# Linear attention beside a squared-ReLU MLP: the reciprocal denominators reach their features by DMA through DRAM instead of by matmuls, and three S groups run in one burst

## The chip, the cores and the metric

The kernel runs on one core of a Trainium2 chip. The metric is device time in microseconds of one execution. TensorE does the matmuls, VectorE and ScalarE read the results out of PSUM, GpSimd (POOL) does adds in SBUF, and SyncE (SP) issues nearly all DMA transfers. PSUM has eight banks of 128 partitions by 512 f32 values, and SBUF holds everything else.

## The reference

The input x is [2048, 448] in bf16. It is normalised per token, without scale or shift, and the result goes into two branches:

```
xn  = layernorm(x)
q, k, v = xn @ wqkv, 16 heads of 28 features;  phi(t) = where(t > 0, t + 1, exp(t)) + 1e-6
kv  = sum over s of phi(k)[s, d] * v[s, e]      per head
z   = sum over s of phi(k)[s, d]                per head
den = phi(q) . z + 1e-6                         per token and head
s   = ((phi(q) @ kv) / den) @ wo
h   = relu(xn @ w1 + b1) ** 2 ;  g = silu(h @ w2 + b2)      1792 hidden features
out = x + s * g
```

There is one denominator for each token and head, 2048 x 16 numbers. Each divides the 28 features of phi(q) of that head, so before the division a number has to be copied to 28 features. That copying is what the change is about.

## The kernel before, in words

**Tiles.** The 2048 tokens are 16 tiles of 128, in four groups of 512. The 448 features are three chunks of 128 and a rest of 64. phi(q) is kept transposed, features on partitions: chunks 0 to 2 in `pqT` (128 x 3 x 2048), the rest in `pqx`, where partitions 0 to 63 hold the even tiles and 64 to 127 the odd ones. phi(k) is kept with tokens on partitions, in `pk`.

**Stages.** The first half normalises, transposes, and runs three kinds of units with the transposed input `xT`: K units (L624, one token tile of phi(k)), Q units (L650, a chunk of phi(q) for one group) and H units (L716, 128 hidden features for one group; L683 adds the bias and takes the ReLU, L697 or L698 squares, into `r2`). Units are packed by fours (`quads`, `pe_four`), two at a time on 64 rows each of the array. Then the attention is folded:

- `qx` (L664) makes the rest features of phi(q); `token_sum` (L785, L791) multiplies xn and phi(k) over all tokens into `at`; `z_cols` (L838) makes z.
- `den` (L883, L890) multiplies phi(q) by z into one bank: partition 32g + h holds head h of token group g. ScalarE takes the logarithm (L905) and exp of its negative (L909): `rden`, the reciprocal denominators, 512 tokens per row.
- `spread(c)` (L921, L927) copies them to features: for each group a matmul of 32 rows of a 0/1 matrix `ehd` with `rden` gives a bank in which each feature's row is its head's row. VectorE multiplies phi(q) by the four banks, in place (L944).
- `fold_wv` (L813) and `fold_wo` (L861) turn `at` into one 448 x 448 matrix `msb`, so that the attention's output is phi(q)/den times `msb`.

Last comes the output, tile by tile. A **gate tile**, `gg(si)` (L957), is 14 matmuls of 448 columns; VectorE evicts it with the bias into `gbuf` (L966), ScalarE applies silu (L999). An **S group**, `ss4` or `ss4_rests_last` (L1026), makes the attention output of four tiles in four banks with 28 matmuls, two at a time. `gate` multiplies an S bank by `gbuf` into `obuf` (L1009), POOL, or VectorE for the last tiles, adds x (L1015), and SP stores the tile. Tiles 12 to 15 are made by `s_tails` (L1082, the rest features, which opens four banks) and `s_main` (L1099). Tile 15 is made in two halves of 224 columns (`gg_part`, L977, L979).

**What sets the order.** Every operation is recorded by `add` with the names it reads and writes, and `schedule` plans all of them on five queues with assumed durations. TensorE and SP keep the order in which the program lists them; on the other engines the planner picks the order. It also gives each PSUM result a bank. Each operation waits for its inputs by semaphores, and every engine works strictly in its planned order. TensorE's list from `den` on is: four H units of group 3, spread 0, fold_wv, gate tile 4, spread 1, fold_wo, tile 5, spread 2, tiles 6 and 7, spread 3, S groups 0 and 1, tiles 8 to 14, S group 2, tails, mains of tiles 12 to 14, tile 15 in halves.

Of the kernel before, what the change touches and what calls it, by code (L numbers as in the profile page):

```python
# [6 lines left out]
ALU = mybir.AluOpType  # L7
AF = mybir.ActivationFunctionType

P = 128  # L10
S, D, F = 2048, 448, 1792
NT, NG, NF = S // 128, S // 512, F // 128
NH, DH = 16, 28
HC = 4
PD = 112
NGB, NOB = 8, 8

LAT = 0.12
PSUM_BANKS = 8
# [280 lines left out]
def bass_recurrent_scan__linear_attn_block__dense_activation_squared_relu__prompt_kernel(  # L300
    nc, A_x, A_wqkv, A_wo, B_x, B_w1, B_b1, B_w2, B_b2, out
):
    with ExitStack() as es:
# [8 lines left out]
        zmask = sb("zmask", [P, 5, 32], f32)  # L312
        ones = sb("ones", [P, 1], bf)
        wz = sb("wz", [P, P], bf)
        ehd = sb("ehd", [P, D], bf)
        x_tok = sb("x_tok", [P, NT, D], bf)
        wqh = sb("wqh", [P, 64], bf)
        xn = sb("xn", [P, NT, 512], bf)
# [19 lines left out]
        eps5 = sb("eps5", [P, 1], f32)  # L338
        r2 = sb("r2", [P, NF, S], bf)
        kvm = sb("kvm", [P, 4, D], bf)  # L340
        msb = sb("msb", [P, 4, D], bf)
        zsb = sb("zsb", [P, 5, 32], bf)
        lnd = sb("lnd", [P, 512], f32)[:, :]
        rden = sb("rden", [P, 512], bf)
# [9 lines left out]
        def free_ap(ap, dims):  # L354
            return bass.AP(tensor=ap.tensor, offset=ap.offset, ap=[ap.ap[0]] + dims)
# [16 lines left out]
        def vset(ap, val, name, again=False, dur=0.08):  # L372
            add("dve", lambda e, _: e.memset(ap, val), [name] if again else [], [name], dur)
# [2 lines left out]
        pr.ops[-1].prio = -1e6  # L376
        vset(hmask[:, :], 1.0, "hmask", dur=0.15)
        vset(zmask[:, :, :], 1.0, "zmask", dur=0.2)
        vset(ehd[:, :], 0.0, "ehd", dur=0.3)
        vset(kvm[:, :, :], 0.0, "kvm", dur=1.0)  # L380
        pool(lambda e, _: e.memset(ones[:, :], 1.0), ["ones"], dur=0.1)
        pool(lambda e, _: e.memset(eps6[:, :], 1e-6), ["eps6"], dur=0.1)
# [12 lines left out]
        def head_masks(after):  # L395
            hv = hmask[:, :].rearrange("p (b j) -> p b j", b=HC)
            select(hv, "hmask", [[-DH, HC], [0, DH]], 0, 1, 0.0, after=after)
            select(hv, "hmask", [[DH, HC], [0, DH]], DH - 1, -1, 0.0, after=after)
            ev = ehd[:, :].rearrange("p (h j) -> p h j", h=NH)
            for g in range(NG):  # L400
                select(ev, "ehd", [[-1, NH], [0, DH]], -32 * g, 1, 1.0, ALU.not_equal, dur=0.6, after=after)

        tok = lambda t, lo, hi: t[0].rearrange("(p s) d -> p s d", s=NT)[:, lo:hi, :]

        def dma(eng, dst, src, writes, nbytes, reads=(), dur=0.45):
            op = add(eng, lambda e, _: e.dma_start(dst, src), reads, writes, dur, nbytes=nbytes)
            if eng == "act":
                op.prio = -1000.0 + len(pr.ops)
# [442 lines left out]
        def fold_wo(c):  # L851
            b = Buf("M")
            hs = {0: (0, 1), 1: (1, 2), 2: (2, 3), 3: (3,)}[c]

            def f(e, _):
                last = None
                for o in range(1 if c < 3 else 2):
                    dst = ps(b)[:, 0:D] if c < 3 else ps(b)[64 * o : 64 * o + 64, 0:D]
                    wd = P if c < 3 else 64
                    for h in hs:  # L860
                        last = e.matmul(  # L861
                            dst, kvm[0:PD, h, c * P : c * P + wd], w_o[0:PD, h, :], start=(h == hs[0]),
                            stop=(h == hs[-1]),
                        )
                return last

            add("pe", f, ["kvd", "kvm", "wo"], [b], 0.19 * len(hs) * (2 if c == 3 else 1))

            def ev(e, eng):
                if eng == "dve":  # L870
                    return e.tensor_copy(msb[:, c, :], ps(b)[:, 0:D])
                return e.activation(out=msb[:, c, :], in_=ps(b)[:, 0:D], func=AF.Copy)

            add("dve", ev, [b], [("msb", c)], 0.62, alts=[("act", 0.55)])

        denb = Buf("DEN")

        def den():
            def f(e, _):
                last = None  # L880
                for c in range(3):
                    for g in range(NG):
                        last = e.matmul(  # L883
                            ps(denb)[32 * g : 32 * g + 32, 0:512], zsb[:, c, :], pqT[:, c, g * 512 : (g + 1) * 512],
                            start=(c == 0), stop=False, skip_group_check=True,
                        )
                for o in (0, 1):
                    for g in range(NG):
                        d4 = ps(denb)[32 * g : 32 * g + 32, o * P : o * P + P]
                        last = e.matmul(  # L890
                            free_ap(d4, [[2 * P, 2], [1, P]]), zsb[:, 3 + o, :],
                            pqx[:, g // 2, 2 * (g % 2) : 2 * (g % 2) + 2, :], start=False, stop=(o == 1),
                            skip_group_check=True,
                        )
# [13 lines left out]
            add(  # L908
                "act", lambda e, _: e.activation(out=rden[:, :], in_=lnd, func=AF.Exp, scale=-1.0), ["lnd"],  # L909
                ["rden"], 0.65,  # L910
            )

        def spread(c):
            bufs = [Buf("RB") for _ in range(NG)]

            def f(e, _):
                last = None
                for g in range(NG):
                    r = slice(32 * g, 32 * g + 32)
                    if c < 3:  # L920
                        last = e.matmul(  # L921
                            ps(bufs[g])[:, 0:512], ehd[r, c * P : (c + 1) * P], rden[r, :], start=True, stop=True
                        )
                    else:
                        for o in (0, 1):
                            d4 = rden[r, o * P : o * P + P]
                            last = e.matmul(  # L927
                                ps(bufs[g])[64 * o : 64 * o + 64, 0:256], ehd[r, 384:448],
                                free_ap(d4, [[2 * P, 2], [1, P]]), start=True, stop=True,
                            )  # L930
                return last

            add("pe", f, ["rden", "ehd"], bufs, 0.22).mode = "row32"
            for g in range(NG):
                if c < 3:
                    sl, n, nm = pqT[:, c, g * 512 : (g + 1) * 512], 512, ("pq", g, c)
                    rd, wr = [nm], [nm]
                else:
                    sl = pqx[:, g // 2, 2 * (g % 2) : 2 * (g % 2) + 2, :].rearrange("p a b -> p (a b)")
                    n = 256  # L940
                    rd, wr = [("pqx", g // 2)], [("pqy", g)]
                add(
                    "dve",
                    lambda e, _, sl=sl, b=bufs[g], n=n: e.tensor_tensor(  # L944
                        out=sl, in0=sl, in1=ps(b)[:, 0:n], op=ALU.mult
                    ),
                    [bufs[g]] + rd, wr, 0.68 if c < 3 else 0.41,
                )

        def gg(si):  # L950
# [265 lines left out]
        for i in range(12, 16):  # L1216
            zsum(i)
        quads("Q2.0 H3.4 Q2.1 H3.6 Q2.2 H3.5 Q3.0 H3.7 Q3.1 H3.12 Q3.2 H3.13")
        qx(0)
        qx(1)  # L1220
        token_sum(3)
# [2 lines left out]
        z_cols()  # L1224
        token_sum(2)
        den()
        quads("H3.8 H3.9 H3.10 H3.11")
        silu_set()
        for si in range(4):
            silu(si)  # L1230
# [25 lines left out]
        s_main(us[3], 3, True, 0, 224)  # L1256
        gg_part(15, 224, D)
# [31 lines left out]
```

## Time and profile before

The median of three executions is 146.9 us (146.82 to 147.07). One more execution was profiled:

| | |
|---|---|
| time of the profiled execution | 146.83 us |
| its span, first to last instruction | 145.1 us |
| granted TensorE clock | 1.0 |
| busy: TensorE, VectorE, ScalarE, POOL | 140.2, 95.7, 78.2, 36.5 us |
| time by queue, of 16 DMA engines | SP's 26.6%, ACT's 0.2% |

The span leaves out 1.7 us around the instructions. Matmuls are pipelined, so the mean of one in the profile (353 ns for 448 columns) is longer than the distance from one to the next; durations of stages are better taken from the chain of work that ended last, which lists stretches without overlap.

### The profile page before, as it was taken

What the parts mean: (1) busy time and instruction counts of PE and PEld (TensorE: products, weight loads), DVE (VectorE), ACT (ScalarE), POOL (GpSimd) and SP (SyncE); (2) the same over time, 40 slices, a digit from 0 to 9 for tenths busy, and PEclk for the clock granted to TensorE, in tenths of its full rate; (3) what the DMA queues carried; (4) which work ended last, traced back from release to release, by engine and by line L of the source; (5) the groups of instructions that cost most, each with busy time, mean ns of one, the idle gap of its engine ahead of it and who ended that gap; (6) DMA issues with size and microseconds to landing.
All of it is one profiled execution on the core that took longest, in us unless ns stands there. A gap on an engine that the chain in (4) does not pass through costs nothing.

```text
span 145.1 us, 2851 instructions
## 1 busy us (share of the span) xinstructions
PE 140.2 (97%) x1134; PEld 72.5 (50%) x1134; DVE 95.7 (66%) x218; ACT 78.2 (54%) x150; POOL 36.5 (25%) x55
## 2 busy tenths in 40 slices
PE   7999999999999999999999999999999999999990
PEld 7774444444455444444444454464444455554490
DVE  5869989899985177678999500089847913123792
ACT  3618897988884198869879412598411012212010
POOL 2123025470000487003540000000000991000590
PEclk9999999999999999999999999999999999999999
DMA  3977899920744100000000000000000232000034
GB/s 94 315 240 234 209 183 374 340 84 0 52 97 103 41 5 0 0 0 5 2 0 0 5 0 0 0 5 2 0 0 0 65 104 88 0 0 0 5 127 127
DMA packets 16025, 10.53 MB, mean 73 GB/s; under 512 B 7500, under 2 KB 15628, under 8 KB 16012
## 3 DMA queue, kind: packets, MB, share of 16 engines
q1 hardware_dynamic: 15824, 10.28, 26.6%
q8 instruction: 9, 0.15, 0.4%
q10 hardware_dynamic: 188, 0.07, 0.2%
q14 instruction: 4, 0.03, 0.1%
HBM read 6.94 MB, written 1.84 MB: 60 GB/s over the span
## 4 chain that ended last, share of the span: by engine, by line
PE 96%; DVE 1%; ACT 1%; issue 0%
PE pb L957 28%; PE pb L716 26%; PE pb L624 7%; PE pb L785 6%; PE pb L650 6%; PE pb L1026 6%; PE pb L712 3%; PE pb L1114 3%; PE pb L979 2%; PE pb L1099 1%; PE pb L664 1%; PE pb L861 1%; PE pb L791 1%; PE pb L921 1%; PE pb L813 1%; PE pb L883 1%
## 5 line engine op out<-in xcount | busy, mean ns | idle before, releaser
L957 PE MATMUL pb<-w,r 128*128 128x448 bf16 x210 | 40.6, 353 | 0.0
L716 PE MATMUL pb<-xT,w 64*128 64x512 bf16 (+1 forms) x291 | 38.3, 376 | 0.0
L683 ACT ACTIVATE r<-pb,b1f 128x512 bf16<-128x512 f32 x54 | 33.7, 691 | 6.7 <-PE pb L716 6.7
L957 PEld LDWEIGHTS pb<-w,r 128*128 128x128 bf16 x210 | 20.2, 98 | 19.5 <-issue 1.2
L1015 POOL TENSOR_TENSOR obuf<-obuf,x_tok 128x448 bf16<-128x448 bf16 x13 | 13.1, 1043 | 53.9 <-DVE obuf L1009 53.9
L999 ACT ACTIVATE gbuf<-gbuf 128x448 bf16<-128x448 bf16 x15 | 8.3, 579 | 26.2 <-DVE gbuf L966 26.1
L716 PEld LDWEIGHTS pb<-xT,w 64*128 64x128 bf16 (+1 forms) x291 | 14.2, 94 | 16.5 <-ACT r L683 0.4
L966 DVE TENSOR_TENSOR gbuf<-pb,b2b 128x448 bf16<-128x448 f32 x15 | 9.4, 625 | 19.3 <-PE pb L957 19.2
L634 POOL TENSOR_TENSOR zacc<-zacc,pk 128x448 f32<-128x448 f32 x13 | 14.5, 1116 | 18.9 <-DVE pk L614 18.4
L697 DVE TENSOR_TENSOR r<-r 128x512 bf16<-128x512 bf16 x37 | 17.4, 502 | 2.0 <-ACT r L683 1.9
L624 PE MATMUL pb<-w_qkv,xT 64*128 64x448 bf16 x112 | 13.2, 349 | 0.0
L944 DVE TENSOR_TENSOR pqT<-pqT,pb 128x512 bf16<-128x512 bf16 x12 | 7.4, 681 | 7.2 <-PE pb L921 7.2
L602 ACT ACTIVATE pk<-pb 128x448 bf16<-128x448 f32 x16 | 7.8, 541 | 7.7 <-PE pb L624 7.7
L698 ACT ACTIVATE r<-r 128x512 bf16<-128x512 bf16 x19 | 11.2, 633 | 0.0
L650 PE MATMUL pb<-xT,w_qkv 64*128 64x512 bf16 x84 | 11.0, 376 | 0.0
L1009 DVE TENSOR_TENSOR obuf<-pb,gbuf 128x448 bf16<-128x448 f32 (+1 forms) x17 | 9.0, 590 | 2.6 <-PE pb L1026 2.4
L716 PE MATMUL pb<-xT,w_1r 64*128 64x512 bf16 x56 | 10.3, 377 | 0.0
L614 DVE SCALAR_TENSOR_TENSOR pk<-pb,pk 128x448 bf16<-128x448 f32 x16 | 9.9, 624 | 0.5
L466 DVE BATCH_NORM_STATS2 st<-x_tok 128x6 f32<-128x448 bf16 x16 | 9.2, 614 | 1.4 <-DMA x_tok<-in_A_x_dram 1.4
L785 PE MATMUL pb<-pk,xn 128*128 128x448 bf16 x48 | 9.4, 353 | 0.0
L607 DVE TENSOR_SCALAR pk<-pk 128x448 bf16<-128x448 bf16 x16 | 6.0, 377 | 4.3 <-ACT pk L602 4.2
L624 PEld LDWEIGHTS pb<-w_qkv,xT 64*128 64x128 bf16 x112 | 5.4, 94 | 6.1 <-issue 0.4
(92 smaller groups left out, 134.5 us busy)
## 6 DMA issues: line engine op xcount, KB each, us to landing
out_dram<-obuf SPq DMA_DIRECT2D x15, 112.0 KB, 1.7
w<-in_B_w_dram SPq DMA_DIRECT2D x1, 1568.0 KB, 9.5
x_tok<-in_A_x_dram SPq DMA_DIRECT2D x3, 448.0 KB, 4.4
w<-in_B_w_dram SPq DMA_DIRECT2D x3, 384.0 KB, 4.2
w_qkv<-in_A_wqkv_dram SPq DMA_DIRECT2D x3, 336.0 KB, 5.6
w_o<-in_A_wo_dram SPq DMA_DIRECT2D x1, 392.0 KB, 8.9
w_qkv<-in_A_wqkv_dram SPq DMA_DIRECT2D x6, 56.0 KB, 5.1
x_tok<-in_A_x_dram SPq DMA_DIRECT2D x2, 112.0 KB, 2.1
```

The source lines that it names most:

```text
L614: lambda e, _: e.scalar_tensor_tensor(out=slot, in0=ps(buf)[:, 0:n], scalar=1.0 + 1e-6, in1=slot, op0=ALU.add, op1=ALU.max),
L624: return e.matmul(ps(b)[:, 0:D], xT[rw, si, c, :], w_qkv[rw, c, D : 2 * D], start=start, stop=stop)
L634: lambda e, _: e.tensor_tensor(out=o[:, 0:D], in0=pk[:, 0, :] if i == 1 else zacc[:, :], in1=pk[:, i, :], op=ALU.add),
L650: return e.matmul(ps(b)[:, 0:512], w_qkv[rw, c, m * P : (m + 1) * P], xT[rw, 4 * g : 4 * g + 4, c, :], start=start, stop=stop,)
L683: rl = lambda e, _: e.activation(out=slot, in_=ps(b)[:, 0:512], func=AF.Relu, bias=b1f[:, fi : fi + 1])
L697: return e.tensor_tensor(out=slot, in0=slot, in1=slot, op=ALU.mult)
L698: return e.activation(out=slot, in_=slot, func=AF.Square)
L716: return e.matmul(ps(b)[:, 0:512], lhs, xT[rw, 4 * g : 4 * g + 4, c, :], start=start, stop=stop, skip_group_check=not full,)
L785: last = e.matmul(ps(b)[:, 0:D], xn[:, si, c * P : (c + 1) * P], pk[:, si, :], start=(si == 0), stop=(si == NT - 1),)
L957: last = e.matmul(ps(b)[:, 0:D], r2[:, fi, si * P : (si + 1) * P], w_2[:, fi, :], start=(fi == 0), stop=(fi == NF - 1),)
L966: lambda e, _: e.tensor_tensor(out=gbuf[:, si % NGB, :], in0=ps(b)[:, 0:D], in1=b2b[:, :], op=ALU.add),
L1015: lambda e, _: e.tensor_tensor(out=ob, in0=ob, in1=x_tok[:, si, lo:hi], op=ALU.add),
```

## The change

The four spread matmuls and the matrix `ehd` go. `rden` is stored to a DRAM scratch `rden_rows` (16 heads x 2 x 1024: even tiles, then odd ones) by four transfers, one per token group; the Exp that makes `rden` writes the even and odd tiles apart. Twelve transfers then load it back, with each head's row repeated for its 28 features, into the space of `pk`, which nobody needs by then; chunk 0 takes two pieces, chunks 1 and 2 three each, and the rest four, because chunks of 128 cut through heads of 28. VectorE multiplies from there: two operations of 1024 columns for each chunk and two of 512 for the rest, instead of twelve of 512 and four of 256 from PSUM.

TensorE's list changes: the four H units come before `qx` instead of after `den`; after `den` come tile 4, fold_wv, tile 5, fold_wo, tiles 6 to 11; then S groups 0, 1, 2 and the tails in one burst; then tiles 12 to 14 and the mains. `gbuf` gets 12 slots and `obuf` 10; to make room `msb` shares the memory of `at`. All three mains of tiles 12 to 14 now have their add on VectorE. The planner's assumed cost of issuing a DMA goes from 0.45 to 0.6.

```diff
-NGB, NOB = 8, 8
+NGB, NOB = 12, 10
-        ehd = sb("ehd", [P, D], bf)
+        rsp = nc.dram_tensor("rden_rows", [NH, 2, 1024], bf)
-        msb = sb("msb", [P, 4, D], bf)
+        msb = at
-        vset(ehd[:, :], 0.0, "ehd", dur=0.3)
-            ev = ehd[:, :].rearrange("p (h j) -> p h j", h=NH)
-            for g in range(NG):
-                select(ev, "ehd", [[-1, NH], [0, DH]], -32 * g, 1, 1.0, ALU.not_equal, dur=0.6, after=after)
-        def dma(eng, dst, src, writes, nbytes, reads=(), dur=0.45):
+        def dma(eng, dst, src, writes, nbytes, reads=(), dur=0.6):
-            add("dve", ev, [b], [("msb", c)], 0.62, alts=[("act", 0.55)])
+            add("dve", ev, [b], [("msb", c), ("at", c)], 0.62, alts=[("act", 0.55)])
-                "act", lambda e, _: e.activation(out=rden[:, :], in_=lnd, func=AF.Exp, scale=-1.0), ["lnd"],
-                ["rden"], 0.65,
+                "act",
+                lambda e, _: e.activation(
+                    out=rden[:, :].rearrange("p (o j t) -> p j o t", o=2, j=2),
+                    in_=lnd.rearrange("p (j o t) -> p j o t", o=2, j=2), func=AF.Exp, scale=-1.0,
+                ),
+                ["lnd"], ["rden"], 0.65,
-        def spread(c):
...
+        rb = pk[:, :, :].rearrange("p a b -> p (a b)")
+        def store_rden():
+            for g in range(NG):
+                dma(
+                    "sp", rsp.ap()[:, :, g * 256 : (g + 1) * 256],
+                    rden[32 * g : 32 * g + NH, :].rearrange("p (o x) -> p o x", o=2), [("rd", g)], NH * 1024, ["rden"],
+                )
+        def load_rden(c):
+            done = [o for o in pr.ops if o.eng in ("pe", "pool") and any(r in o.reads for r in [("pk", NT - 1)])]
+            def piece(p0, h, n, reps, cols, src0, name):
+                src = bass.AP(tensor=rsp, offset=h * 2048 + src0, ap=[[2048, n], [0, reps], [1, cols]])
+                o = 2048 * c
+                dma("sp", rb[p0 : p0 + n * reps, o : o + cols], src, [name], n * reps * cols * 2, [("rd", g) for g in range(NG)])
...
+            for half in range(1 if c < 3 else 2):
...
+                while f < f1:
+                    h = f // DH
+                    n = (f1 - f) // DH if f % DH == 0 else 0
+                    reps = DH if n else min((h + 1) * DH, f1) - f
...
+                    piece(p0 + f - f0, h, n, reps, cols, src0, ("rb", c, half, k))
...
+        def divide(c):
+            for v in (0, 1):
+                if c < 3:
+                    sl = pqT[:, c, v * 1024 : (v + 1) * 1024].rearrange("p (j o t) -> p j o t", o=2, t=P)
+                    o = 2048 * c + v * 512
+                    r = free_ap(rb[:, o : o + P], [[P, 4], [1024, 2], [1, P]])
...
+                else:
+                    sl = pqx[:, v, :, :].rearrange("p a b -> p (a b)")
+                    r = rb[:, 6144 + 512 * v : 6656 + 512 * v]
...
+                    "dve", lambda e, _, sl=sl, r=r: e.tensor_tensor(out=sl, in0=sl, in1=r, op=ALU.mult), rd + names[c], wr,
...
         quads("Q2.0 H3.4 Q2.1 H3.6 Q2.2 H3.5 Q3.0 H3.7 Q3.1 H3.12 Q3.2 H3.13")
+        quads("H3.8 H3.9 H3.10 H3.11")
         qx(0)
...
         den()
-        quads("H3.8 H3.9 H3.10 H3.11")
+        store_rden()
+        for c in range(4):
+            load_rden(c)
         silu_set()
...
-        spread(0)
+        ggs(4)
         fold_wv()
-        ggs(4)
-        spread(1)
+        ggs(5)
         for c in range(4):
             fold_wo(c)
-        ggs(5)
-        spread(2)
         ggs(6)
-        ggs(7)
-        spread(3)
-        ss4_rests_last(0)
+        for si in range(7, 12):
+            ggs(si)
+        for c in range(4):
+            divide(c)
+        ss4(0)
         ss4(1)
-        for si in range(8, 15):
-            ggs(si)
         ss4(2)
         us = s_tails([(12, 0, D), (13, 0, D), (14, 0, D), (15, 0, D)])
+        for si in range(12, 15):
+            ggs(si)
         for k in range(3):
-            s_main(us[k], k, k > 0)
+            s_main(us[k], k)
```

More of the change, by code (lines that the diff above doesn't have):

```diff
@@ L908, in den @@
             add(
-                "act", lambda e, _: e.activation(out=rden[:, :], in_=lnd, func=AF.Exp, scale=-1.0), ["lnd"],
-                ["rden"], 0.65,
-            )
-        def spread(c):
[L914 to L933, printed above, removed]
-            for g in range(NG):
+                "act",
@@ new lines, in load_rden @@
+        def load_rden(c):
[4 more added lines that the diff above has]
+                dma("sp", rb[p0 : p0 + n * reps, o : o + cols], src, [name], n * reps * cols * 2, [("rd", g) for g in range(NG)])
+                pr.ops[-1].deps.update(done)
+                for d in done:
+                    d.succ.append(pr.ops[-1])
+            for half in range(1 if c < 3 else 2):
+                f0, p0, k = P * c, 64 * half, 0
+                f1 = f0 + (P if c < 3 else 64)
+                cols, src0 = (2048, 0) if c < 3 else (1024, 1024 * half)
+                f = f0
+                while f < f1:
+                    h = f // DH
+                    n = (f1 - f) // DH if f % DH == 0 else 0
+                    reps = DH if n else min((h + 1) * DH, f1) - f
+                    if f % DH == 0 and n == 0:
+                        reps = f1 - f
+                    n = max(n, 1)
+                    piece(p0 + f - f0, h, n, reps, cols, src0, ("rb", c, half, k))
+                    f += n * reps
+                    k += 1
+                names[c] = names.get(c, []) + [("rb", c, half, i) for i in range(k)]
@@ L935, in spread @@
+        names = {}
+        def divide(c):
+            for v in (0, 1):
                 if c < 3:
-                    sl, n, nm = pqT[:, c, g * 512 : (g + 1) * 512], 512, ("pq", g, c)
-                    rd, wr = [nm], [nm]
-                else:
-                    sl = pqx[:, g // 2, 2 * (g % 2) : 2 * (g % 2) + 2, :].rearrange("p a b -> p (a b)")
-                    n = 256
-                    rd, wr = [("pqx", g // 2)], [("pqy", g)]
-                add(
[L943 to L947, printed above, removed]
+                    sl = pqT[:, c, v * 1024 : (v + 1) * 1024].rearrange("p (j o t) -> p j o t", o=2, t=P)
+                    o = 2048 * c + v * 512
+                    r = free_ap(rb[:, o : o + P], [[P, 4], [1024, 2], [1, P]])
+                    rd = wr = [("pq", g, c) for g in (2 * v, 2 * v + 1)]
+                else:
+                    sl = pqx[:, v, :, :].rearrange("p a b -> p (a b)")
+                    r = rb[:, 6144 + 512 * v : 6656 + 512 * v]
+                    rd, wr = [("pqx", v)], [("pqy", 2 * v), ("pqy", 2 * v + 1)]
+                add(
+                    "dve", lambda e, _, sl=sl, r=r: e.tensor_tensor(out=sl, in0=sl, in1=r, op=ALU.mult), rd + names[c], wr,
+                    0.78 if c < 3 else 0.42,
```

## The prediction

> **What bounds the kernel now.** I read the page's totals first, then the chain of work that ended last.
>
> ```profile
> span 145.1 us, 2851 instructions
> PE 140.2 (97%) x1134; PEld 72.5 (50%) x1134; DVE 95.7 (66%) x218; ACT 78.2 (54%) x150; POOL 36.5 (25%) x55
> PE 96%; DVE 1%; ACT 1%; issue 0%
> ```
>
> TensorE carries 96% of the chain (third line), so a matmul removed is time gained, unless TensorE then waits. Next the chain in order of time (start, us, what) around the edit:
>
> ```profile
> 77.64 1.85 PE pb L664 x16
> ...
> 91.07 0.22 PE pb L890 x8
> 91.29 3.13 PE pb L716 x28
> 94.42 0.33 PE pb L921 x4
> 94.74 0.96 PE pb L813 x16
> 95.70 2.65 PE pb L957 x14
> 98.35 0.33 PE pb L921 x4
> 98.68 1.55 PE pb L861 x8
> 100.23 2.75 PE pb L957 x14
> ...
> 108.72 0.25 PE pb L927 x8
> 108.96 5.45 PE pb L1026 x56
> ...
> 135.81 0.38 PE pb L1082 x4
> 136.19 1.81 PE pb L1099 x9
> 138.00 0.10 PE pb L977
> ```
>
> A gate tile (L957) costs 2.65 us alone and 2.75 after another tiling of the array: each switch costs 0.10. The spreads (L921, L927) stand directly on the chain. Then the tail, from the timeline (start, us):
>
> ```profile
> 137.97 3.16 POOL L1015 TENSOR_TENSOR obuf<-obuf,x_tok 128x448 bf16<-128x448 bf16 x3
> 142.02 0.28 DVE L1015 TENSOR_TENSOR obuf<-obuf,x_tok 128x224 bf16<-128x224 bf16 x1
> 142.99 0.45 SPq L406 DMA_DIRECT2D out_dram<-obuf  x1
> ```
>
> The last add ends at 142.30, but its store is issued at 142.99: SP takes stores in order, and those behind POOL's last add (ended 141.13) go out some 0.48 apart. That is 0.67 us of queue at the end. Last, the DMA part:
>
> ```profile
> q10 hardware_dynamic: 188, 0.07, 0.2%
> out_dram<-obuf SPq DMA_DIRECT2D x15, 112.0 KB, 1.7
> ```
>
> A store lands 1.7 us after its issue. Queue 10 (ACT's) had three transfers: b1r with 14 rows and two w_1r pieces of 64: 142 data packets. The other 46 are 14 + 16 + 16[...].
>
> [...] The trace shows slow matmuls only in the warm-up at the start (36 in 4.02 us)[...]. [...] VectorE's 448-column adds beside POOL took 1,070 ns, the 224-column ones 270.
>
> **The change part by part.** TensorE. Up to 77.64 its order is unchanged. The group of four H units (28 matmuls, 3.13 with its switch, 3.02 without) moves ahead of qx, so den ends at 91.29 + 3.02 = 94.31. Its banks are free by then: the Q phi that holds one of them ended at 76.91. From there, by the rows above: gate tile 4, 2.75; fold_wv 0.86 (0.96 less the switch); tile 5, 2.65; fold_wo 1.45; tiles 6 to 11, 2.75 + 5 x 2.65 = 16.00, ending at 118.02. The S burst: a switch and 84 matmuls, 8.05 (28 took 2.65); tails 0.38; tiles 12 to 14, 8.05; s_main 1.71 without its switch. It ends at 136.2, against 138.0: **1.80 us off TensorE**, of which the spreads are 0.33 x 3 + 0.25 = 1.24 and the rest are switches.
>
> Tail. POOL's last add is now that of tile 11 and ends before tile 14; tiles 12 to 14 are added on VectorE. So SP's queue is empty when the last add ends: **0.67 us** (between 0.4 and 0.7; VectorE gets one full add more, but then has no POOL beside it, and has the last tile's other half to make up lateness).
>
> DMA, all on SP's queue. rden was ready at 92.69 and is now at 95.71. Four stores, 0.5 apart, the last issued at 97.2 and landed 1.7 later: 98.9. All twelve loads wait for all four stores. They bring 384 rows of 4,096 B and 128 of 2,048 B, 1.84 MB. Over 16 engines at the 374 GB/s of the page's fullest slice that is 4.9 us. But the source patterns are 4 heads x 28 copies for chunks 0 and 1, 3 x 28 for chunk 2, 2 x 28 twice for chunk 3, against 112, 84 and 56 partitions[...]. Engine 0 then gets 28+1, 1+28+1 and 2+28+2 rows of 4 KB, 91, and 2 x (1+28) = 58 of 2 KB. The packet records of before show 140 ns for 3,584 B and 74 for 1,792 B; the line through both gives 159 for 4,096 and 83 for 2,048. Sum 91 x 0.159 + 58 x 0.083 = 19.3 us. With 0.9 us from issue to first packet and 0.2 to the semaphore, both read from the output stores' packets, chunk 3 lands at **119.3**; chunks 0, 1, 2 at about 104.7, 109.4, 114.5. Bounds: pipelined packets at the line's slope alone (151 ns) give 118.1; the 3,584 B packets under full load came one per 167 ns and engine, 190 for 4 KB, which gives 123.
>
> VectorE. Removed: 12 multiplies of 681 ns and 4 of 414 from PSUM. Added: six of 128x1024 and two of 128x512, all in SBUF. The nearest row is the 128x512 square, 418 ns[...]. VectorE works in order, and its order in the changed kernel is: chunk 0 both halves, tile 7's eviction, chunk 1 first half, chunk 2 first half, tile 8's eviction, chunk 3's first half (the rest features), chunks 1 and 2 second halves, tile 9's eviction, chunk 3's second half, tiles 10 and 11. So while VectorE waits for chunk 3, the evictions of tiles 9 to 11 queue behind; TensorE doesn't notice, since those three tiles have banks of their own. The first S group needs chunk 3's first half: 119.3 + 0.42 + 0.1 = 119.8, where TensorE is ready at 118.1: **a stall of 1.7 us**. After it VectorE owes 1.3 + 0.62 + 0.4 + 1.24 = 3.6 us and reaches S's first gate at 123.3, 1.2 after that was ready. Gates take 0.57 against TensorE's 0.66 a tile, so it catches up; two bank waits of about 0.1 remain (second S1 pair behind tile 11's eviction, tile 12 behind a gate): 0.2.
>
> At nothing: removing the ehd memset and four selects (POOL 25% busy); msb laid over at (fold_wo writes 3 us after fold_wv read it); gbuf 12 and obuf 10 deep (gates 10 and 11 wait for the stores of tiles 0 and 1, landed some 3 us before); the strided Exp. Their cover is idle time on POOL, ACT and VectorE, and without it each costs below 0.3.
>
> Sum: -1.80 - 0.67 + 1.7 + 0.2 = -0.57. The profiled execution took 146.83, the median is 146.9: **146.3**.
>
> **The rivals.** *All engines serve the loads.* If the split follows the destination's partitions, everything lands by about 108, ten us early: 146.9 - 2.47 = 144.4. [...]
> *Slow few engines, ending slower.* The same wait, but each 4 KB packet takes over about 164 ns, or the twelve transfers leave gaps on engine 0. At 164 the stall, 2.5, eats the whole gain; at 190, chunk 3 lands at 123.0, the stall is 5.5, 144.4 + 5.6 = 150.0[...]. For it: the 167 ns under load, and every engine reads the same row 28 times. Against: only four engines draw on the memory here, where 16 did.
> *The burst is bound by gates.* Twelve tiles need 6.8 us of gates and VectorE enters with tile 11's eviction; if gates slow to over 0.66, tile 12 waits: about 1 us on top of 144.4. The gates of before, beside POOL's adds as here, kept 0.57.
>
> **How the numbers follow.** Forecast 0.48 (own range 145.0 to 147.3), all engines 0.20, slow engines 0.27, gates or another small wait 0.05. The smallest change that a measurement here can tell from none is 0.2%, 146.6 to 147.2. Below it: 0.34 of the forecast, 0.19 and 0.02: 0.55. Within: 0.09, 0.02 and 0.01: 0.12. Above: 0.33, mostly the slow engines. The range goes from 144.2, just below the all-engine case, to 149.5, which leaves the worst of the slow engines, about 0.12, outside.
>
> **What would show it.** Right: TensorE idle 1 to 2.5 us before the first S group, released by VectorE, which waited for the last load; the loads at some 100 GB/s from 100 to 119; landings growing to 10 us and more; the last store issued within 0.1 of the last add. Wrong: loads done by 110 and no idle (first rival), packets well over 160 ns (second), idle inside the burst (third), or idle between den and tile 11, which I put at none.

## The result and the profile after

The changed kernel takes 153.74 us in the median of six executions (152.91 to 154.65), against 146.86 us (146.67 to 147.07) for the kernel before: a ratio of 1.0469, with a 95% interval of 1.0422 to 1.0515. It is slower by 6.9 us. The predicted 146.3 us is wrong, and its range, 144.2 to 149.5, does not hold the result either.

The profiled execution of the changed kernel took 154.65 us, the slowest of the six; what follows is read from it. Line numbers are those of the changed kernel: a gate tile is L975, an S group L1044, a division L964, a DMA issue L402. First the page's totals, the two rows of 40 slices that changed most (a slice is 3.8 us), and the shares of the chain:

```profile
span 152.6 us, 2814 instructions
PE 140.8 (92%) x1114; PEld 73.3 (48%) x1114; DVE 91.3 (60%) x212; ACT 77.1 (51%) x148; POOL 32.8 (22%) x50
PEclk9999999999999999999999999999999965999999
GB/s 94 329 201 222 167 262 373 273 50 24 118 16 122 0 4 0 0 0 4 0 0 4 0 0 0 18 17 108 103 101 77 55 25 4 35 86 150 90 71 53
PE 76%; DMA 10%; SPq 8%; ACT 1%; DVE 1%; issue 1%
```

TensorE was 96% of the chain and is now 76%; transfers and their issue have taken 18%. The granted clock, whose mean was 1.0 before, falls to 0.6 and 0.5 in slices 33 and 34, shortly before and in the S burst. And just before that, the transfer rate comes down in steps, 108, 103, 101, 77, 55, 25 GB/s: by the packet records the loads' packets run mostly four at a time from 108.3 to 114.2, then three to 118.9, then two to 123.2. The chain in order of time (start, us, what) has the whole story:

```profile
95.20 0.64 ACT rden L906
...
97.21 0.59 SPq L402
...
97.84 2.75 DMA rden_rows<-rden
...
100.61 0.74 SPq L402
...
107.90 3.88 SPq L402
...
111.82 13.17 DMA pk<-rden_rows
...
125.01 0.44 DVE pqx L964
...
125.50 10.21 PE pb L1044 x63
...
136.08 8.05 PE pb L975 x42
144.14 1.70 PE pb L1117 x9
```

`rden` is ready at 95.84. Its four stores are issued one after another and the last lands at 100.59. Only then do the twelve loads go out, and the last of them lands at 124.99. The eleventh of these issues took 3.88 us, but the packets of the loads ran on beside it, at 100 to 102 GB/s from 108 to 112. VectorE divides (0.44), and TensorE starts the S burst at 125.50. Tile 11 had ended at 118.10. The waits of TensorE and of VectorE in this stretch (us in total, times, longest) say the same:

```profile
PE pb L1044 <- DVE pqx L964: 7.4, 1, 7.4
DVE pqT L964 <- DMA pk<-rden_rows: 12.2, 3, 4.7
DVE pqx L964 <- DMA pk<-rden_rows: 3.6, 1, 3.6
```

The burst itself, 84 matmuls of which the chain lists 63, then takes 10.21 us; at full clock the same 84 take 8.05, as in the runs below. These stretches (bounds; us; busy time of TensorE, its weight loads, VectorE, ScalarE, POOL; granted clock; DMA share; GB/s) show why:

```profile
121.00:123.00 2.00, 0.00 (x0) 0.00 (x0) 0.43 (x1) 0.58 (x1) 0.00 (x0) 0.99 0.13 49
123.00:125.00 2.00, 0.00 (x0) 0.00 (x0) 0.00 (x0) 0.00 (x0) 0.00 (x0) 0.50 0.07 25
...
127.00:129.00 2.00, 2.00 (x14) 0.86 (x12) 1.57 (x4) 1.50 (x3) 0.00 (x0) 0.50 0.04 8
129.00:131.00 2.00, 2.00 (x20) 0.86 (x16) 1.17 (x3) 0.18 (x1) 0.47 (x1) 0.81 0.00 0
131.00:133.00 2.00, 2.00 (x24) 1.03 (x22) 1.51 (x3) 0.00 (x0) 2.00 (x3) 1.00 0.18 57
```

The last matmul of tile 11 ends at 118.10; by the clock records the granted clock falls to 0.5 at 122.95, after 4.85 idle microseconds, and stays there until 129.78, the first 4.3 us of the burst: 14 matmuls in 2 us where 24 fit at full clock. Last the tail, from the timeline:

```profile
149.85 0.27 DVE L1033 TENSOR_TENSOR obuf<-obuf,x_tok 128x224 bf16<-128x224 bf16 x1
150.16 0.33 SPq L402 DMA_DIRECT2D out_dram<-obuf  x1
```

The last store is issued as soon as the last add has ended.

The two profiled executions differ by 154.65 - 146.83 = 7.82 us. The last S matmul of tiles 12 to 14 ends at 145.84 instead of 138.00, which is +7.84: 7.40 of idle time, 2.16 of half clock (10.21 - 8.05), and -1.72 of TensorE work that is gone. From there to the end of the span it is 6.73 us instead of 7.10 (-0.37), and outside the span 2.08 instead of 1.73 (+0.35).

### The profile page after: what moved, and what is told of

The parts are those of the page before. It is cut to its first block, busy times and chain, and to the rows that moved or that the text cites. A ratio compares the mean times of both kernels' runs of the same rounds, so it can differ in the third digit from the quotient of the medians.

```text
span 152.6 us, 2814 instructions
## 1 busy us (share of the span) xinstructions
PE 140.8 (92%) x1114; PEld 73.3 (48%) x1114; DVE 91.3 (60%) x212; ACT 77.1 (51%) x148; POOL 32.8 (22%) x50
## 4 chain that ended last, share of the span: by engine, by line
PE 76%; DMA 10%; SPq 8%; ACT 1%; DVE 1%; issue 1%
PE pb L712 25%; PE pb L975 12%; DMA pk<-rden_rows 9%; SPq L402 8%; PE pb L620 7%; PE pb L1044 7%; PE pb L781 6%; PE pb L646 6%; PE pb L708 3%; PE pb L1132 3%; DMA rden_rows<-rden 2%; PE pb L997 2%; PE pb L1117 1%; PE pb L660 1%; PE pb L787 1%; PE pb L742 1%
## 5 line engine op out<-in xcount | busy, mean ns | idle before, releaser
L975 PE MATMUL pb<-w,r 128*128 128x448 bf16 x210 | 40.6, 353 | 0.0
L975 PEld LDWEIGHTS pb<-w,r 128*128 128x128 bf16 x210 | 20.2, 98 | 19.5 <-issue 0.8
L1033 POOL TENSOR_TENSOR obuf<-obuf,x_tok 128x448 bf16<-128x448 bf16 x12 | 11.9, 1039 | 56.3 <-DVE obuf L1027 56.3
L630 POOL TENSOR_TENSOR zacc<-zacc,pk 128x448 f32<-128x448 f32 x13 | 14.6, 1126 | 22.0 <-DVE pk L610 18.9
L1044 PE MATMUL pb<-at,pqT 64*128 64x448 bf16 x72 | 9.8, 409 | 7.4 <-DVE pqx L964 7.4
L964 DVE TENSOR_TENSOR pqT<-pqT,pk 128x1024 bf16<-128x1024 bf16 x6 | 4.0, 688 | 12.2 <-DMA pk<-rden_rows 12.2
L1044 PEld LDWEIGHTS pb<-at,pqT 64*128 64x128 bf16 x72 | 3.8, 108 | 12.3 <-DVE pqx L964 7.8
```

The source lines that it names most:

```text
L630: lambda e, _: e.tensor_tensor(out=o[:, 0:D], in0=pk[:, 0, :] if i == 1 else zacc[:, :], in1=pk[:, i, :], op=ALU.add),
L975: last = e.matmul(ps(b)[:, 0:D], r2[:, fi, si * P : (si + 1) * P], w_2[:, fi, :], start=(fi == 0), stop=(fi == NF - 1),)
L1033: lambda e, _: e.tensor_tensor(out=ob, in0=ob, in1=x_tok[:, si, lo:hi], op=ALU.add),
L1044: return e.matmul(ps(b)[:, 0:D], lhs, msb[rw, c, :], start=start, stop=stop)
```

## The experiments

My theory after this reading: the work on TensorE and the tail changed as predicted, and the whole loss is the landing of the last load, 125 instead of 119.3, with the idle time and the half clock that follow from it. The rivals to be told apart from it: that the traffic or the new order slows something else too; that the half clock has another cause than the idle time; and, for the landing, whether few engines, slow packets or the start of the queue make it late.

### No wait for the loads

```diff
-                    r = free_ap(rb[:, o : o + P], [[P, 4], [1024, 2], [1, P]])
+                    r = free_ap(w_2[:, :, :].rearrange("p a b -> p (a b)")[:, o : o + P], [[P, 4], [1024, 2], [1, P]])
...
-                    "dve", lambda e, _, sl=sl, r=r: e.tensor_tensor(out=sl, in0=sl, in1=r, op=ALU.mult), rd + names[c], wr,
+                    "dve", lambda e, _, sl=sl, r=r: e.tensor_tensor(out=sl, in0=sl, in1=r, op=ALU.mult), rd + ["w2", ("g", 6)], wr,
```

The multiplies read weights that are long there, instead of the loaded rows, those of the rest features too. Stores and loads still run, and the end of the program waits for them; the division is left out.

> The changed kernel with all four stores and twelve loads still issued, but the eight multiplies read a tile of w_2 that has lain in SBUF since the first third of the run, from tile 6 on, instead of the loaded rows (so the division is left out). Theory, that the whole loss is the wait for the loads and what follows from it: TensorE goes from tile 11 straight into the S burst at 118.1, its clock stays at 1.0, and the gain of the other parts shows: about 2.1 us under the kernel before, 144.7. Rival, that the burst, the shared at or the new end cost time of their own: it stays above 147, with idle inside the burst or after it.

Measured: 144.86 us (144.63 to 144.94), a ratio of 0.9859 [0.9845, 0.9872]. Its chain:

```profile
101.90 15.99 PE pb L975 x84
117.90 8.05 PE pb L1044 x84
```

No idle, full clock, and the burst takes 8.05. The loads ran until 123.6 beside it and cost nothing that the chain shows. So wait and clock are the whole loss: without them the change would gain 2.1 us.

### Idle time filled with matmuls

```diff
+        def filler(n):
+            def f(e, _):
+                last = None
+                for _i in range(n):
+                    last = e.matmul(ps(fb)[:, 0:512], wz[:, :], r2[:, 0, 0:512], start=True, stop=True)
+                return last
+
+            add("pe", f, ["wz", ("r2", 0, 0)], [fb], 0.3)
+
+        filler(30)
```

Thirty matmuls whose result nobody reads stand between tile 11 and the burst; the wait for the loads stays.

> The changed kernel with 30 matmuls of 512 columns, whose result nobody reads, between tile 11 and the S burst: 6.5 us of work in a wait of 7.4. The wait is as long as before. Theory, that the idle array lost its clock: the S burst runs at full clock, 8.1 us instead of 10.2, and the time falls by about 2.1, to 151.6. Rival, that the burst's matmuls were slow for another reason (VectorE and ScalarE catching up, or operands just written): the burst stays at 10.2 and the time at 153.7.

Measured: 152.04 us (151.46 to 152.6), ratio 1.0349 [1.0315, 1.0384]. Chain:

```profile
118.05 6.47 PE pb L1273 x30
124.53 8.05 PE pb L1044 x84
```

The burst stands behind 6.5 us without useful work, nearly as much as in the changed kernel (7.4 us), and yet runs in 8.05. The half clock came from the idleness, and keeping the array busy is worth 1.7 us of the median (153.74 to 152.04), though it computes nothing. The 1.7 is less than the 2.16 of the burst. In this execution chunk 3 landed at 123.3 and its first half was divided at 123.70, so the filler, which ended at 124.52, itself held the burst up by some 0.8 us.

### Single heads on two queues

```diff
-                dma("sp", rb[p0 : p0 + n * reps, o : o + cols], src, [name], n * reps * cols * 2, [("rd", g) for g in range(NG)])
+                dma(("sp", "act")[turn[0] % 2], rb[p0 : p0 + n * reps, o : o + cols], src, [name], n * reps * cols * 2, [("rd", g) for g in range(NG)])
+                turn[0] += 1
...
-                    piece(p0 + f - f0, h, n, reps, cols, src0, ("rb", c, half, k))
-                    f += n * reps
-                    k += 1
+                    for i in range(n):
+                        piece(p0 + f - f0, h + i, 1, reps, cols, src0, ("rb", c, half, k))
+                        f += reps
+                        k += 1
...
```

Every transfer brings one head, 22 instead of 12, issued by SP and ScalarE in turn. The bytes are the same.

> The changed kernel with each load cut into single heads (22 transfers of up to 28 rows, source 1 x 28 rows, on SP and ACT by turns), same bytes. Theory, that the number of engines is what the outer dimension of the source allows[...]; the issues (11 a queue, 0.65 each) are what is left, the last load lands near 110, TensorE doesn't wait: 144.7. Rival, that the loads are slow because many packets read one row of DRAM: [...]the last landing stays at 120 or later and the time above 149.

Measured: 144.76 us (144.63 to 145.17), ratio 0.9863 [0.9847, 0.9880]. One of its stretches, and two lines of its chain:

```profile
106.00:108.00 2.00, 2.00 (x12) 1.00 (x11) 1.85 (x3) 0.00 (x0) 0.00 (x0) 1.00 0.91 197
```

```profile
102.00 16.00 PE pb L977 x84
118.00 8.05 PE pb L1046 x84
```

The DMA engines are 0.91 busy here at 197 GB/s, where the changed kernel keeps to 100 GB/s, and the last packet is over at 111.8: 13 us earlier, by splitting transfers. The last load landed at 112.7, later than the 110 that I had expected, but early enough. The kernel beats the changed one by 9.0 us and the one before, 146.97 beside it, by 2.2, and equals the run without the wait.

### Single heads on SP alone

As above, but all 22 on SP's queue (the lines below are set against those of the run above).

```diff
-                dma(("sp", "act")[turn[0] % 2], rb[p0 : p0 + n * reps, o : o + cols], src, [name], n * reps * cols * 2, [("rd", g) for g in range(NG)])
+                dma("sp", rb[p0 : p0 + n * reps, o : o + cols], src, [name], n * reps * cols * 2, [("rd", g) for g in range(NG)])
```

> Twenty-two transfers of one head each, as in the run with single heads, but all on SP's queue. Theory (the count of engines that serve a load decides, not the second queue): 22 issues of 0.65 us from 100.6 end at about 115, the last lands 2 to 3.5 us later, 117 to 118.5, stall 0 to 1 us, time 144.8 to 146. Rival (the gain came from issuing on two queues): the landing stays near 125 us and the time near 153.

Measured: 146.16 us (145.72 to 146.25), ratio 0.9957 [0.9939, 0.9974]; the kernel before took 146.67 beside this run and the next three. Chain:

```profile
115.93 0.74 SPq L402
...
116.71 2.33 DMA pk<-rden_rows
...
119.06 0.43 DVE pqx L966
...
119.55 8.12 PE pb L1046 x84
```

Landing, idle time and time lie just above the ranges that I gave. Now the issues are the bound, 0.55 to 0.90 us each, and the last one, begun at 116.71, is followed by the landing after 2.3. So most of the gain comes from the transfers of one head, not from the second queue; the second queue is worth the 1.4 us of idle time that is left here. That idle time did not lower the clock: it stays granted at 1.00, and the burst takes 8.12.

### At most two heads

```diff
-                    piece(p0 + f - f0, h, n, reps, cols, src0, ("rb", c, half, k))
-                    f += n * reps
-                    k += 1
+                    while n:
+                        m = min(n, 2)
+                        piece(p0 + f - f0, h, m, reps, cols, src0, ("rb", c, half, k))
+                        f, h, n, k = f + m * reps, h + m, n - m, k + 1
```

> The four-head and three-head transfers of chunks 0 to 2 are split into transfers of at most two heads. By the theory that a transfer of n heads is read by n engines, the first engine then carries 58 rows of 4 KB more, 58 x 0.16 = 9.3 us: chunk 3 lands near 134 us instead of 125, the stall is near 16.7 us instead of 7.4, and the time 153.7 + 9.3 = 163. Rival (the landing is set by the total of bytes, or by the start of the queue): landing within 2 us of 125, time 152 to 156.

Measured, in one run: 162.33 us. From the timeline, the first division of each chunk, with what it waited for:

```profile
113.28 1.29 DVE L965 TENSOR_TENSOR pqT<-pqT,pk 128x1024 bf16<-128x1024 bf16 x2 [7.83 <-DMA pk<-rden_rows]
122.64 1.29 DVE L965 TENSOR_TENSOR pqT<-pqT,pk 128x1024 bf16<-128x1024 bf16 x2 [7.52 <-DMA pk<-rden_rows]
128.16 1.29 DVE L965 TENSOR_TENSOR pqT<-pqT,pk 128x1024 bf16<-128x1024 bf16 x2 [3.69 <-DMA pk<-rden_rows]
132.78 0.43 DVE L965 TENSOR_TENSOR pqx<-pqx,pk 128x512 bf16<-128x512 bf16 x1 [3.33 <-DMA pk<-rden_rows]
```

Splitting four heads into two and two makes the loads later, splitting them into ones makes them earlier. From 117 to 131 the DMA share is 0.13 to 0.15 of the 16 engines, at 48 to 57 GB/s: two engines' worth. If each of the two takes one head's 28 rows, and the second pair follows the first, chunk 1 needs 56 rows of 4 KB, 56 x 0.159 = 8.9 us; the trace has 9.36 from chunk 0 to chunk 1. Chunk 2 has one pair, 28 rows, 4.5; the trace has 5.52, with the third head and two parts of heads beside it.

### Without the small transfers

```diff
-                    piece(p0 + f - f0, h, n, reps, cols, src0, ("rb", c, half, k))
+                    if reps == DH:
+                        piece(p0 + f - f0, h, n, reps, cols, src0, ("rb", c, half, k))
+                        k += 1
                     f += n * reps
-                    k += 1
```

The seven transfers of parts of a head are left out: the heads 4, 9 and 13, which the chunks cut through, 84 of the 448 features.

> The seven transfers that hold only part of a head (16, 12, 4, 24, 20, 8 and 8 features) are left out, so those features are multiplied by what lay in the buffer before and the output is not the reference's; five transfers of two to four heads stay. The first engine's share falls only by 7 rows of 4 KB and 2 of 2 KB, 1.3 us. Theory A (the first packets are slow, 0.3 to 1.0 us, because the small transfers put many more engines on the same rows): the slow first packets go, the landing is at 102.4 + 18.0 = 120.4 us, the stall some 2.7 us with no drop of the clock, time near 147.5. Theory B (the start is slow whatever is in the queue): landing 123.5 to 124, stall near 6, clock drop stays, time near 152.

Measured, in one run: 151.38 us. Timeline of the divisions, and chain:

```profile
107.73 0.69 DVE L965 TENSOR_TENSOR pqT<-pqT,pk 128x1024 bf16<-128x1024 bf16 x1 [2.21 <-DMA pk<-rden_rows]
112.13 0.69 DVE L965 TENSOR_TENSOR pqT<-pqT,pk 128x1024 bf16<-128x1024 bf16 x1 [3.71 <-DMA pk<-rden_rows]
116.57 0.69 DVE L965 TENSOR_TENSOR pqT<-pqT,pk 128x1024 bf16<-128x1024 bf16 x1 [3.21 <-DMA pk<-rden_rows]
121.21 0.42 DVE L965 TENSOR_TENSOR pqx<-pqx,pk 128x512 bf16<-128x512 bf16 x1 [3.95 <-DMA pk<-rden_rows]
```

```profile
103.45 17.73 DMA pk<-rden_rows
...
121.69 10.86 PE pb L1045 x84
```

The landing, 121.2, is nearer theory A (120.4) than theory B (123.5 to 124). The packet records, in the table, agree: the slow packets are nearly gone. But they also correct A's size. The profiled execution of the changed kernel was the slowest of its six; in three other runs with the same twelve transfers the excess over the bare packets (the stretch from first packet to landing, less the 91 and 58 rows that the prediction counts, or 84 and 56 without the small transfers, at 159 and 83 ns) is 1.6 to 2.1 us, and here it is still 1.2.

| run | first packet | landing of chunk 3 | excess, us | 4 KB packets over 250 ns |
|---|---|---|---|---|
| the changed kernel | 102.1 | 125.0 | 3.6 | 70 of 384 |
| no wait | 102.2 | 123.6 | 2.1 | 50 |
| filled | 102.3 | 123.3 | 1.6 | 36 |
| late burst, below | 101.7 | 123.0 | 2.0 | 43 |
| without the small transfers | 102.0 | 121.2 | 1.2 | 5 of 308 |

The time was missed for another reason: I expected an idle stretch of 2.7 us without a drop of the clock. It was 3.6 us, and the clock fell: the burst took 10.86, the longest of all.

### The burst behind tile 14

```diff
-NGB, NOB = 12, 10
+NGB, NOB = 15, 10
...
-        for si in range(7, 12):
+        for si in range(7, 15):
             ggs(si)
...
-        for si in range(12, 15):
-            ggs(si)
```

> The twelve loads as in the changed kernel; the gate buffer has 15 slots instead of 12 and the burst of S groups stands behind gate tile 14 instead of tile 11, so that 3 x 2.67 = 8.0 us more of TensorE work cover the landing at 125.0 us. Theory (the late landing of chunk 3 is the whole loss): the burst begins at 118.1 + 8.0 = 126.1 us with its operand there, no idle window, granted clock 1.0, time 144.9 (the run without the waits) plus up to 2 us for the additions of tiles 12 to 14, which now queue on VectorE behind the multiplies: 145 to 147. Rival (the loads also slow the engines around them, or land later when more work runs beside them): a stall remains, 150 or more.

Measured: 148.41 us (147.98 to 149.49), ratio 1.0128 [1.0082, 1.0174]. The burst and an addition in its chain, and two stretches:

```profile
125.86 8.05 PE pb L1044 x84
...
136.78 2.34 DVE obuf L1033 x2
```

```profile
123.00:127.00 4.00, 4.00 (x30) 1.94 (x29) 3.99 (x8) 1.50 (x3) 0.00 (x0) 1.00 0.00 0
135.00:139.00 4.00, 4.00 (x39) 3.54 (x37) 3.98 (x6) 0.36 (x1) 4.00 (x5) 1.00 0.40 129
```

As the theory has it, idle time and half clock are gone. The time is still 1.4 us above the upper end that I gave. Now VectorE is the bound: it is busy 3.99 of 4 us when the divisions come, behind them queue the evictions of the extra gate tiles and the gates of the burst, and at 135 to 139 both VectorE and POOL are full. From 135.07 on the chain runs over VectorE instead of TensorE. TensorE's wait was covered with work whose followers then came too late.

### Matmul spreads in the new order

The four matmul spreads, `ehd` and the divisions from PSUM are put back, after fold_wv, fold_wo, tile 6 and tile 7; the changed order, the burst and the tail stay, and there are no transfers of `rden`.

```diff
-        store_rden()
-        for c in range(4):
-            load_rden(c)
...
+        spread(0)
...
+        spread(1)
...
-        for si in range(7, 12):
+        spread(2)
+        ggs(7)
+        spread(3)
+        for si in range(8, 12):
             ggs(si)
-        for c in range(4):
-            divide(c)
```

> The DMA part undone, the order kept: spreads by matmul as before (after fold_wv, fold_wo, tile 6 and tile 7), but the H units ahead of qx, three S groups and the tails in one burst between tiles 11 and 12, adds of tiles 12 to 14 on VectorE. Of the 1.8 us on TensorE the spreads take back 1.24 and some 0.4 of switches, so TensorE is 0.2 shorter than in the kernel before; the end, where SP's queue is empty, gives 0.35. Theory, that the order is harmless: 146.3, faster by 0.3 to 0.5%. Rival, that the burst of twelve gates holds TensorE up: 147 or more.

Measured: 145.8 us (145.55 to 146.03), ratio 0.9926 [0.9913, 0.9938]. Chain:

```profile
98.17 0.33 PE pb L922 x4
98.50 2.75 PE pb L958 x14
...
119.81 8.05 PE pb L1027 x84
...
136.29 1.70 PE pb L1100 x9
```

The mains of tiles 12 to 14 end at 137.99, as before the change (138.00): what the burst saves in switches, the spreads between gate tiles cost again (a tile takes 2.75 after each). What the profiled execution gains over that of the kernel before, 0.8 us, therefore lies behind that point: its span from there is 6.3 us instead of 7.1. By the medians the gain is 1.2 us. I had expected 0.2 from TensorE and 0.35 from the end; why the end gives more is not shown. And the spreads by DMA, where they don't wait, are worth 145.80 - 144.76 = 1.0 us against the matmuls.

## Why the prediction was wrong

**TensorE: right.** In the run without the wait the mains end at 136.08, predicted 136.2; tile 11 ended at 118.10, predicted 118.02, in the changed kernel itself. The burst at full clock took 8.05 as predicted, and neither bank waits (put at 0.2) nor the rival of gates that bound the burst showed: there is no idle inside it.

**Tail: in part.** SP's queue is empty as said, but the span goes on 2.4 us after the last store's issue, where it was 2.1 before, and the span gains 0.37 of the 0.67. In the seven other runs that end in this order the stretch behind the mains is 0.37 to 0.79 shorter than before. Outside the span the profiled executions of this study took 1.7 to 2.4 us, without a pattern that I could find, and where it was over 2 that took back much of the gain. Free of idle time the kernel takes 144.76 to 144.86, predicted 144.4.

**Few engines, and their steady packets: right.** That a load has as many engines as heads, 4, 4, 3 and 2, and that the next one waits for the same engines, the prediction assumes; no trace of before shows it. For the number, see the last two columns of these stretches of the changed kernel, the share of the 16 DMA engines and the GB/s:

```profile
110.00:112.00 2.00, 2.00 (x12) 1.06 (x11) 1.80 (x3) 0.00 (x0) 0.00 (x0) 1.00 0.26 102
...
116.00:118.00 2.00, 2.00 (x12) 0.88 (x9) 0.00 (x0) 0.00 (x0) 0.00 (x0) 1.00 0.20 80
...
120.00:122.00 2.00, 0.00 (x0) 0.00 (x0) 1.23 (x2) 0.54 (x1) 0.00 (x0) 1.00 0.13 49
```

Of 16 engines, 0.26, 0.20 and 0.13 are 4.2, 3.2 and 2.1. That the loads follow each other is in the landings: without the small transfers, the chunks land 4.40, 4.44 and 4.64 us apart, and 28 x 0.159 = 4.45 and 56 x 0.083 = 4.65. What the small transfers add to an engine, 7 of the 91 rows and 2 of the 58, is assumed too; with them, chunk 3 lands 14.81 us after chunk 0 instead of 13.48, 1.3 more. In the changed kernel, too, everything from chunk 0 on keeps to the plan: chunks 0 to 3 are divided at

```profile
110.20 1.29 DVE L964 TENSOR_TENSOR pqT<-pqT,pk 128x1024 bf16<-128x1024 bf16 x2 [4.68 <-DMA pk<-rden_rows]
...
115.28 0.69 DVE L964 TENSOR_TENSOR pqT<-pqT,pk 128x1024 bf16<-128x1024 bf16 x1 [3.25 <-DMA pk<-rden_rows]
120.20 0.69 DVE L964 TENSOR_TENSOR pqT<-pqT,pk 128x1024 bf16<-128x1024 bf16 x1 [4.23 <-DMA pk<-rden_rows]
```

and at 125.01: 14.8 us from chunk 0 to chunk 3, where 104.7 to 119.3 had 14.6.

**The step that failed: "chunk 3 lands at 119.3".** Nearly all of the lateness, 5.5 of 5.7 us, is there at chunk 0 (110.2 instead of 104.7); from there on the arithmetic of the rows holds. These terms of the sum were too small:

- "Four stores, 0.5 apart, the last issued at 97.2 and landed 1.7 later: 98.9". The last was issued at 97.84 and landed 2.75 after its issue, at 100.59: **+1.7**. I had taken both terms from the output stores.
- "0.9 us from issue to first packet", also an output store's. The first load's packets came 1.5 us after its issue: **+0.6**.
- The 4 KB packets were priced from the first at 159 ns. In steady state their median is 159 to 161, but in the first six microseconds up to 1.0 us: **+3.1** in the profiled execution, by its packet records (the last 4 KB packet ended 17.6 us after the first began; 91 x 0.159 = 14.5). In the other runs of the same transfers it is 1 to 1.7.
- "0.2 to the semaphore". The last packet ended at 124.50, the landing is 124.99: **+0.3**. The 2 KB packets themselves took the planned 4.8.

The bound of 123 that I gave was one of the rate; no term before the first packet had a bound at all.

What ran when the stores landed late is in the records. The first two of the four landed 1.95 and 1.84 us after their issue, near the 1.7; the others took 3.22 and 2.75. The profile's page lists, beside the queues of SP and ACT, a queue of another kind, with nine packets of 16 KB:

```profile
q8 instruction: 9, 0.15, 0.4%
```

One of them runs from 98.23 to 99.35, and the last completion packets of the late stores start 0.11 and 0.23 us after its end. It is so in all eight runs with these stores: the packet lasts 0.93 to 1.47 us, and a late completion starts 0.10 to 0.13 after its end. The four stores left 64 completion packets; 62 had started by 99.34, and the two late ones are the last. That the 16 KB packet held them back is my reading; no run isolates it, but the kernel before shows the same: another such packet ran from 114.33 to 115.56, and the three output stores issued at 113.33, 114.32 and 115.31 landed 3.43, 2.78 and 2.09 us after their issue. The median of 1.7, from which I priced, hides them.

**The second step: the price of the idle time.** I put one microsecond of idle for one of lateness, and had no measured price for a fallen clock: in the kernel before, the granted clock is 1.0 from 6.5 us to the end. It cost 2.16. By the clock records of the runs the half clock lasted 6.83 us in the changed kernel and without the small transfers, and 17.07 in the run of two heads, and from restart to recovery the burst loses just half of the time:

| run | idle | clock falls | burst starts | clock back | half of it | burst over 8.05 |
|---|---|---|---|---|---|---|
| single heads on SP | 118.1 to 119.55 | no | 119.55 | | 0 | 0.07 |
| without the small transfers | 118.1 to 121.7 | 120.46 | 121.69 | 127.29 | 2.80 | 2.81 |
| the changed kernel | 118.1 to 125.5 | 122.95 | 125.50 | 129.78 | 2.14 | 2.16 |
| two heads | 118.0 to 133.3 | 121.06 | 133.26 | 138.13 | 2.43 | 2.45 |

So the price is a step in these runs: 0.07 us at 1.4 us of idle, and 2.81, 2.16 and 2.45 at 3.6, 7.4 and 15.2, not growing with its length. The clock fell 2.4, 4.9 and 3.0 us after TensorE had stopped, and came back 5.6, 4.3 and 4.9 us after the burst had started. What sets these delays is not shown, and between 1.4 and 3.6 us of idle nothing was run.

With the 144.86 of the run without the wait the account closes. Idle time and the excess of the burst added to it give 146.4, 151.3, 154.4 and 162.5 us for the four rows of the table; their profiled executions took 146.21, 151.38, 154.65 and 162.33.

**The rivals.** *All engines serve the loads* is refuted by the shares of 0.26, 0.20 and 0.13, but the run with single heads realises it: 144.76, predicted 144.4. *Slow few engines, ending slower*, at 150.0, had 0.27 and the right shape (late landing, long idle, fallen clock), with the wrong cause. In the mean its condition held: 17.6 us for 91 rows are 193 ns a row, and 171 to 178 in three other runs of these transfers. But its grounds, load on the memory and a row read 28 times, would slow every packet, and the packets were on time (159 to 161 ns) once the first six microseconds were over. The result lies 3.7 us beyond it because the landing, 125.0, was later than its 123 and the half clock added 2.16 in the profiled execution. The range failed at its upper end for the same two terms. The 6.9 us between the medians are, then, 144.86 - 146.86 = -2.0 us for the change itself, measured without the wait (-2.1 against the 146.97 beside that run), and 153.74 - 144.86 = +8.9 for idle time and half clock (7.40 + 2.16 = 9.6 in the profiled execution, which took 0.9 more than the median).

What stays open: why the first packets are slow. That many engines read the same few rows at once fits the runs (in the changed kernel 16 packets ran at a time at 104.5, 4 at 108.5; 70, 50, 36 and 43 slow packets with the small transfers, 5 without; 255 of 384 with single heads on two queues and 127 on one, where all the same everything landed early). The run of two heads speaks against the mere start of the queue and the mere number of transfers in flight: 22 of its 39 slow packets start between 114 and 116, in the middle of the stream, just after a transfer of one whole head had been issued (from 110.13 to 114.13). Of the 122 packets between 106 and 114, with some eight transfers under way as well, one is slow. No run varies the number of engines on a row alone. That the scatter of the changed kernel, 1.7 us against 0.4 for the one before, comes from these packets is argued, not shown.

## What to carry to other kernels

A transfer whose source repeats rows may keep only a few engines busy: those of four, three and two heads here ran at shares of 0.26, 0.20 and 0.13 of the 16 engines (102, 80 and 49 GB/s), those of one head, on two queues, at up to 0.91 (197 GB/s). Count the rows of one busy engine, not the bytes over all 16, and choose the split by the measured share (here one head at a time, which on two queues turned a loss of 6.9 us into a gain of 2.2). When a round trip through DRAM is to be hidden, price its start from the single landings of the profile and not from their median, or give it a wide bound, since stores, issue and first packets made 5.5 us of error here and the streaming part 0.2. And an idle stretch of TensorE of a few microseconds must not be priced by its length alone: 3.6 us of it cost 2.8 us more here, 7.4 us 2.2 more, and 1.4 us 0.07.

## What was new about the hardware

- Splitting transfers works in both directions: four heads in one transfer landed chunk 3 at 125.0, two by two at 132.8, one by one at 119.0 on one queue and 112.7 on two.
- The loads still in flight beside the S burst cost TensorE nothing (8.05 us with and without them), and even 91% busy DMA engines left the gate tiles at 16.00 us for six.
- Beside a 16 KB packet of the instruction queue, stores landed 2.75 and 3.22 us after issue (16 KB each, changed kernel) or 2.09 to 3.43 (112 KB, kernel before); without one, 1.84 and 1.95, and 1.7 in the median.
- The granted clock fell to 0.5 after 2.4 us of idle TensorE (without the small transfers), 3.0 (two heads) and 4.9 (changed kernel), and not in 1.4 us (single heads on SP); it came back 4.3 to 5.6 us after the burst's start.
